# Attention's small products visit TensorE two head pairs at a time, and the first stage's plan counts blocks of instructions

## The chip, the core and the metric

The kernel runs on one core of a Trainium2 chip. Five engines work side by side there and meet through semaphores: TensorE (PE in the profile; its weight loads are shown apart as PEld), VectorE (DVE), ScalarE (ACT), GpSimd (POOL) and SyncE (SP), which issues the transfers from and to HBM. The metric is the time of one execution on the device in microseconds (us). The kernel before took 953.29, 954.51 and 958.97 us in three runs; the median, 954.51 us, is its time.

## The reference: what is computed

Attention with a narrow window over 8 batches, 8 heads, 576 positions and 64 features, followed by a feed-forward layer with a GELU:

```
scores = scale * np.matmul(q, k.transpose(0, 1, 3, 2))
mask_plain = (rel >= 0) & (rel < window)                                              # window = 32
mask_dil = (rel >= 0) & (rel < window * dilation) & (rel % dilation == 0)             # dilation = 4
attn = np.exp(scores - max) ;  attn = attn / (np.sum(attn, axis=-1, keepdims=True) + 1e-09)
x = (attn @ v), heads side by side: 4608 tokens of 512 features
h = x @ w_in                                 # 512 -> 2048
g = 0.5 * h * (1.0 + erf(h / sqrt(2)))
out = g @ w_out                              # 2048 -> 512
```

The first four heads use the plain window, the last four the dilated one; in a dilated head the positions are sorted by their remainder, so that its window is narrow too. Attention is little arithmetic in many small products, the feed-forward layer much arithmetic in large ones.

## The kernel before

**Tiling.** The tokens are worked in nine chunks of 512. Chunks 0 to 7 take the first 512 positions of a batch each; chunk 8 takes the 64 remaining positions of all eight batches. A chunk has four *head pairs* (two plain, two dilated). For a pair, `scores` multiplies blocks of 32 queries by 64 keys (L310), `lowest` and `softmax` make the exponentials on DVE and ACT, `norm` and `turn` divide and transpose on DVE, `av` multiplies by the values in products of 32 columns (L459; L451 for the dilated pairs of chunk 8, called *wide*, with 96 keys a query), and `xout` brings the result out of PSUM as two float32r parts, the value rounded by an ACT cast (L487) and the remainder by a DVE subtraction (L490).

The feed-forward layer keeps all weights in SBUF, each as two float32r parts. `ffn_h` (L501) and `ffn_o` (L516) run three products for every product of the reference, 128 rows by 512 columns each. Such a row of twelve products is called a *unit* below; a chunk has 16 units of `ffn_h` and 16 of `ffn_o`, 384 products in all.

A product of `scores` or `av` has float32 operands, and the trace shows it as two MATMULs and two LDWEIGHTS; a product of the feed-forward layer and a transpose on PE are one of each. So the row `x128` of the built program below is `x256` in the trace for small products, and `x128` is `x128` for large ones.

**The order in chunks 1 to 8** is written by hand. While the feed-forward layer of chunk c runs, the attention of chunk c+1 is put between its units by a list of steps, each with a position: position 2 is behind the second `ffn_h` unit, and from 24 to 32 a position counts quarters, three `ffn_o` products each. `A_SC` gives the position of `scores` for all four pairs, `A_X` that of `av`. So PE gets two *visits* of attention in a chunk: the scores of four pairs, 128 products one behind the other, and the value products of four pairs, 128 products or, for chunk 8, 64 and 192 wide ones.

**The first stage** (attention of chunks 0 and 1, splitting of the weights, feed-forward layer of chunk 0) is ordered by `Plan`. A job gives the engine and an estimated time of each of its steps; `Plan.run` takes, again and again, the step that can begin first by its own clock, shifted by a rank (`RANK`), and writes it into its engine's queue. `ORDER` is the order of the loads on SP. A weight arrives as 64-bit floats and is split by DVE in five or six instructions (L213 to L227) and by one ACT cast (L232). A weight in `TWICE` is loaded a second time, two bytes further on (`mid_w`), and needs one instruction less on DVE (L217). Of the first `HALVED` weights each half is split by itself.

On PE the first stage also has `turn_pe` (transposes of chunk 1, L399), `av_one` (value products of chunk 1, L413) and, for chunk 0, `av` in another shape (L429).

Of the kernel before, what the change touches and what calls it, by code (L numbers as in the profile page):

```python
# [18 lines left out]
P = 128  # L19
# [14 lines left out]
TWICE = (1, 2, 4, 7, 11, 12, 15)  # L34

HALVED = 2
# [3 lines left out]
LATE, LATE_PE, COLD = 0.25, 0.55, 38  # L40
KAPPA, AHEAD = 2.4e-05, 5
ORDER = ("q0 q1 Q0 q2 w0 q3 Q1 v0 m1 v2 m2 Q2 w1 w3 w2 w4 V0 m4 Q3 w8 w6 w5 w9 m7 w7 w11 V2 w10 m11 w14 w12 "
         "m12 w13 m15 w15")
RANK = dict(att0=-3340, split=10720, high=-3120, gelu=-7400, o=7030, scores=(-220, 1980), low=(-4680, -3170, -1270,
            -280), exp=(-220, -170, 2700, 1170), norm=(2990, 750, 2180, -840), t=(2990, 3130, 2240, 1480), av=(-7400,
            -7240), x=(-5520, -2430, -1090, -4980), store=5000)


class Plan:
# [5 lines left out]
    def __init__(self, rings):  # L55
        self.rings = {n: [0.0] * k for n, k in rings.items()}
        self.jobs, self.done, self.free = [], {}, {"DMA": 1.9}
        self.table = "exp"

# [16 lines left out]

    def run(self):
        while self.jobs:
            best = None
            for j in self.jobs:  # L80
# [7 lines left out]
                for n, t in ops.items():  # L88
                    e, _, table = n.partition("/")
                    at = max(r - (LATE if j.get("on") == e != "PE" else 0.0), self.free.get(e, 0.0))  # L90
                    end = at + t + (1.3 if table not in ("", self.table) else 0.0)
                    if e == "PE" and at < COLD:
                        end += 0.6 * t
                    choices.append((end, at, e, table))
                end, at, e, table = min(choices)
                key = (round(at + KAPPA * j["rank"], 2), j["rank"])
                if best is None or key < best[0]:
                    best = (key, j, e, at, end, table)
            _, j, e, at, end, table = best
# [18 lines left out]
def at_once(gen):  # L118

    e = None  # L120
    try:
        while True:
            e = next(iter(gen.send(e))).partition("/")[0]
# [5 lines left out]
def attn_ffn(ctx: ExitStack, tc: tile.TileContext, qk, qk_lp, qk_ld, v_0, v, v_ld, w, outT):  # L129
# [12 lines left out]
    masks = const.tile([P, NU + 1, 2 * KB], F32, name="masks")  # L142
    two_masks = const.tile([P, KL], F32, name="two_masks")
# [145 lines left out]
    def scores(s, bank):  # L289

        yield {"PE": 0.75}
# [21 lines left out]
    def lowest(s):  # L313
# [8 lines left out]
        if s.c < 2:  # L322
            yield {"DVE": 0.6}
            nc.vector.tensor_reduce(s.st[:, 0].rearrange("p (h u) -> p h u", h=2),  # L324
                                    s.sc[:, :, s.at:s.at + n].rearrange("p h (u k) -> p h u k", u=NU), axis=AX.X, op=ALU.max)
            yield {"DVE": 0.08}
# [22 lines left out]
    def softmax(s):  # L349
        for i in range(2 * NU):  # L350
            if i % 4 == 0 and s.c == 0 or i == 0:
                yield {"ACT/exp": 1.32 if s.c == 0 else 2.64}
# [4 lines left out]

    def norm(s, on="DVE"):
        t = s.st[:, 1]
        yield {"DVE": 0.08}  # L360
        nc.vector.tensor_scalar_add(t, t, EPS)
        yield {"DVE": 0.1}
        nc.vector.reciprocal(t, t)
# [4 lines left out]
        elif on == "ACT":  # L368
            yield {"ACT": 1.6}
# [25 lines left out]
    def turn_pe(s, bank):  # L395

        yield {"PE": 0.9}
# [402 lines left out]
```

## Time and profile before

| | |
|---|---|
| time, median of 3 runs | 954.51 us (953.29 to 958.97) |
| the profiled execution | 953.56 us, its span 951.8 us |
| PE busy | 889.0 us, 93% of the span, 8408 MATMULs |
| DVE, ACT busy | 359.5 us (38%), 373.6 us (39%) |
| POOL busy | 9.6 us (1%) |
| HBM | 62.91 MB read, 9.44 MB written, 76 GB/s over the span |
| chain that ended last | PE 88%, issue 4%, ACT 3%, DVE 3%, DMA 1% |

The profile's times are of one execution. In a row of the timeline the first number is the start of a group of instructions in us from the span's start, the second the group's length; at its end, in brackets, stand the idle time ahead of it and what ended that. "issue" there means that the engine waited for nothing that the profile shows. The length of a group holds the modelled end of its last product, so what a row of products costs is read from start to start. PEclk is the share of TensorE's clock that the throttle granted. A busy share is a mean over the span; what the change is worth is read place by place.

The first stage lasts to about 152.6 us, where the first two `ffn_h` units of chunk 1 begin. The chunks 1 to 7 follow with some 100 us each, and chunk 8, beside which no attention stands, ends at 948.1 us.

### The profile page before, as it was taken

The numbers are of one execution on the slowest core, as the hardware profiler recorded it, in microseconds if no ns is written. First come the engines' busy times: TensorE is split into PE (matmuls) and PEld (weight loads), VectorE is DVE, ScalarE is ACT, GpSimd is POOL, SyncE is SP. The second block draws the span as 40 slices with busy tenths as digits, with TensorE's granted clock in tenths as the row PEclk, the third lists the DMA queues.
The fourth block names the chain that finished last, engine by engine and source line by source line (L and its number), as shares of the span: only waits on it lengthen the run. The fifth ranks groups of instructions, "written<-read, shape, count | busy, mean of one in ns | idle before, by whom it ended". The sixth has DMA issues, their size and how long they took to land.

```text
span 951.8 us, 19064 instructions
## 1 busy us (share of the span) xinstructions
PE 889.0 (93%) x8408; PEld 733.4 (77%) x8408; DVE 359.5 (38%) x608; ACT 373.6 (39%) x1017; POOL 9.6 (1%) x48
## 2 busy tenths in 40 slices
PE   4588997999999999999999999999999999989998
PEld 3367886888878877887788778877787888778886
DVE  3597991362136212622163205421462155211020
ACT  5458442453236422732272316331443254323040
POOL 4000000000000000000000000000000000000000
PEclk9579999999999999999999999999999999979999
DMA  9962415000320032003300140005000430000001
GB/s 374 390 245 93 176 64 214 9 0 2 132 91 1 1 123 101 1 1 112 112 1 1 54 170 1 1 3 186 35 0 2 144 133 24 2 24 22 1 1 45
DMA packets 16643, 73.58 MB, mean 77 GB/s; under 512 B 1840, under 2 KB 2096, under 8 KB 12336
## 3 DMA queue, kind: packets, MB, share of 16 engines
q1 hardware_dynamic: 16560, 72.36, 20.7%
q8 instruction: 66, 1.08, 0.5%
q14 instruction: 17, 0.14, 0.0%
HBM read 62.91 MB, written 9.44 MB: 76 GB/s over the span
## 4 chain that ended last, share of the span: by engine, by line
PE 88%; issue 4%; ACT 3%; DVE 3%; DMA 1%; POOL 0%; SPq 0%; POOLq 0%; ACTq 0%; DVEq 0%
PE ps L516 41%; PE ps L501 40%; PE ps L459 3%; PE ps L310 3%; ACT sm L355 1%; DMA raw_qk<-qk 1%; PE ps L429 1%; PE ps L451 1%; DMA raw_w<-w 0%; PE ps L296 0%; DVE raw_w L221 0%; DVE weight L227 0%; DVE st L324 0%; DVE x L490 0%; ACT x L487 0%
## 5 line engine op out<-in xcount | busy, mean ns | idle before, releaser
L501 PE MATMUL ps<-x,weight 128*128 128x512 f32 x1728 | 408.3, 396 | 7.6 <-ACT weight L232 7.6
L516 PE MATMUL ps<-g,weight 128*128 128x512 f32 x1728 | 408.5, 396 | 0.0
L501 PEld LDWEIGHTS ps<-x,weight 128*128 128x128 f32 x1728 | 329.8, 191 | 78.3 <-ACT weight L232 8.5
L516 PEld LDWEIGHTS ps<-g,weight 128*128 128x128 f32 x1728 | 329.9, 192 | 69.8
L511 DVE TENSOR_TENSOR g<-gf,g 128x512 fp32r<-128x512 f32 x144 | 99.6, 692 | 432.7 <-ACT g L509 432.7
L506 ACT ACTIVATE gf<-ps 128x512 f32<-128x512 f32 x144 | 86.1, 598 | 336.1 <-PE ps L501 335.9
L509 ACT CAST g<-gf 128x512 fp32r<-128x512 f32 x144 | 89.4, 621 | 4.6
L355 ACT ACTIVATE sm<-sm,st 128x64 f32<-128x64 f32 (+1 forms) x224 | 74.9, 337 | 0.1
L185 ACT COPY o_sb<-ps 128x512 f32<-128x512 f32 (+1 forms) x35 | 20.3, 581 | 124.5 <-PE ps L516 123.7
L490 DVE TENSOR_TENSOR x<-ps,x 128x512 fp32r<-128x512 f32 (+1 forms) x40 | 31.7, 809 | 87.2 <-ACT x L487 78.3
L487 ACT CAST x<-ps 128x512 fp32r<-128x512 f32 (+1 forms) x40 | 29.5, 771 | 78.8 <-PE ps L459 38.1
L310 PE MATMUL ps<-raw_qk 64*32 64x64 f32 (+1 forms) x2304 | 31.3, 239 | 17.4 <-issue 15.2
L392 DVE STREAM_TRANSPOSE turned<-sm 32x256 f32<-32x256 f32 x104 | 45.4, 436 | 2.0
L310 PEld LDWEIGHTS ps<-raw_qk 64*32 64x32 f32 x2304 | 26.5, 111 | 23.6 <-issue 21.6
L355 ACT ACTIVATION_READ_ACCUMULATOR sm<-sm,st 128x1 f32 x224 | 42.1, 188 | 0.0
L459 PE MATMUL ps<-turned,v_sb 64*64 64x32 f32 x1664 | 28.1, 223 | 7.7 <-issue 7.7
L459 PEld LDWEIGHTS ps<-turned,v_sb 64*64 64x64 f32 x1664 | 26.7, 138 | 10.7 <-issue 10.7
L232 ACT CAST weight<-raw_w 128x1024 fp32r<-128x1024 f32 (+1 forms) x18 | 18.8, 1051 | 15.3 <-DVE raw_w L221 15.3
L355 ACT ACTIVATE sm<-ps,st 128x64 f32<-128x64 f32 x64 | 19.0, 329 | 7.2 <-PE ps L310 5.7
L387 DVE STREAM_TRANSPOSE turned<-sm 128x512 f32<-128x512 f32 x30 | 21.3, 710 | 0.9
L374 DVE TENSOR_TENSOR sm<-sm,st 128x512 f32<-128x512 f32 x30 | 20.7, 692 | 1.0
L221 DVE SCALAR_TENSOR_TENSOR raw_w<-raw_w,spare 128x1024 uint32<-128x1024 uint32 (+1 forms) x18 | 19.9, 1105 | 0.5
(51 smaller groups left out, 238.8 us busy)
## 6 DMA issues: line engine op xcount, KB each, us to landing
raw_qk<-qk SPq DMA_DIRECT2D x32, 512.0 KB, 6.0
raw_w<-w SPq DMA_DIRECT2D x16, 1024.0 KB, 8.0
v_sb<-v SPq DMA_DIRECT2D x15, 1024.0 KB, 5.0
outT<-o_sb SPq DMA_DIRECT2D x35, 256.0 KB, 2.2
mid_w<-w SPq DMA_DIRECT2D x7, 1023.5 KB, 6.4
raw_qk<-qk_ld SPq DMA_DIRECT2D x2, 1024.0 KB, 7.7
v_wide<-v_ld SPq DMA_DIRECT2D x2, 768.0 KB, 6.3
v<-v SPq DMA_DIRECT2D x2, 640.0 KB, 13.3
```

The costliest lines, as they stand in the source:

```text
L310: nc.tensor.matmul(s.sc[32 * r:32 * r + 32, h, c0:c0 + s.nk], x[:, q0:q0 + 32], x[:, k0:k0 + s.nk], start=s.c > 1, stop=s.c > 1 or u == NU ...
L355: nc.scalar.activation(t, s.sc[:, i // NU, at:at + 2 * KB] if s.c < 2 else t, AF.Exp, bias=s.st[:, 0, i:i + 1], scale=SCALE if s.c < 2 els ...
L387: nc.vector.transpose(s.t.rearrange("p i j b -> p (i j b)"), s.all.rearrange("p i k -> p (i k)"))
L392: nc.vector.transpose(s.t[32 * to:32 * to + 32, :, r % 2], s.all[32 * r:32 * r + 32, :, j * KB:(j + 1) * KB])
L459: nc.tensor.matmul(px(r)[h * D:(h + 1) * D, u * KB:(u + 1) * KB], s.v[rows, u, j, h * D:(h + 1) * D], s.t[rows, h * NU + slot(s, u), j], s ...
L487: nc.scalar.copy(h, y)
L490: nc.vector.tensor_sub(l, y, h)
L501: nc.tensor.matmul(bank, weights[f][:, t, cc * P:(cc + 1) * P], x[:, xx], start=n == 0, stop=n == 3 * NC - 1)
L506: nc.scalar.activation(gf, bank, AF.Gelu)
L509: nc.scalar.copy(g[:, 0], gf)
L511: nc.vector.tensor_sub(g[:, 1], gf, g[:, 0])
L516: nc.tensor.matmul(ps[:, d], weights[f][:, t, DM + d * P:DM + (d + 1) * P], gs[f][:, u], start=f == 0 and n == 0, stop=f == NF - 1 and n == 2)
```

## The change

Three things are changed.

1. In chunks 1 to 7 the attention steps are spread over more visits. `scores` of pairs 0 and 1 stays at position 2, that of pairs 2 and 3 goes to position 4; `av` of pairs 0 and 1 stays at 24.75, that of pairs 2 and 3 goes to 26.75, and their `xout` behind it. The wide `av` of chunk 8 is cut in halves of 96 MATMULs (`u0`), 18 or 3 feed-forward products apart. `lowest`, `softmax`, `norm`, `turn` and the loads keep their positions.
2. `Plan` has another model of PE: `on_pe` counts instructions in blocks of 256, lets a block be there a fixed time after the block ahead of it began, and makes PE slower for 4.5 us after a pause. Steps on PE give their number of instructions ("PE:132"). Some estimated times on DVE and ACT are new, and the sum and its inverse are a step of their own (`inverse`).
3. `TWICE` now has ten weights (3, 5, 6, 7, 8, 10 to 14) instead of seven (1, 2, 4, 7, 11, 12, 15), `HALVED` is 3 instead of 2, and `ORDER` and `RANK` have other entries. `gate` is new but not reached: `ORDER` has no entry that begins with n.

```
-TWICE = (1, 2, 4, 7, 11, 12, 15)
+TWICE = (3, 5, 6, 7, 8, 10, 11, 12, 13, 14)
-HALVED = 2
+HALVED = 3
-LATE, LATE_PE, COLD = 0.25, 0.55, 38
+BLOCK, FIRST, FETCH, FETCH_BUSY = 256, 63, 4.2, 5.9
+SLOW, WARM, IDLE = 0.8, 4.5, 1.5
-ORDER = ("q0 q1 Q0 q2 w0 q3 Q1 v0 m1 v2 m2 Q2 w1 w3 w2 w4 V0 m4 Q3 w8 w6 w5 w9 m7 w7 w11 V2 w10 m11 w14 w12 "
+ORDER = ("q0 q1 Q0 q2 v2 q3 Q1 m5 w2 v0 w0 w1 w3 w4 Q2 Q3 V0 V2 m3 w5 w7 m7 m6 m10 w6 m8 w9 w8 m11 w12 m13 w10 "
...
+    def on_pe(self, at, t, n, keep):
+        busy = at if at - self.free.get("PE", 0.0) > IDLE else self.busy
+        there, count, begin = dict(self.there), self.n, at
+        while n > 0:
+            k = count // BLOCK
+            begin = max(begin, there[k])
+            if k + 1 not in there:
+                there[k + 1] = begin + (FETCH if self.free["DMA"] < begin + 1 else FETCH_BUSY)
+            some = min(n, (k + 1) * BLOCK - count)
+            d = t * some / n
+            begin, t = begin + d * (1 + (SLOW if begin < busy + WARM else 0)), t - d
+            count, n = count + some, n - some
+        if keep:
+            self.there, self.n, self.busy = there, count, busy
+        return begin
...
-        yield {"PE": 0.75}
+        yield {"PE:132": 1.15}
...
-    def av(s, px):
+    def av(s, px, u0=0):
...
-            for u in range(NU):
+            for u in range(u0, u0 + 2):
...
-    A_SC, A_LOW, A_E, A_N, A_X, A_QK, A_V = 2, 2.5, 8.5, 10.5, 24.75, 26.5, 3
+    A_SC, A_E, A_N, A_X, A_QK, A_V = (2, 4), 8.5, 10.5, (24.75, 26.75), 26.5, 3
...
-            add(c, A_SC if not wide else 8.25, 1, scores(s[p], bank))
-            add(c, A_LOW + p if not wide else 8.5 + (p - 2), 2, lowest(s[p]))
+            add(c, A_SC[p // 2] if not wide else 8.25, 1, scores(s[p], bank))
+            add(c, A_SC[p // 2] + .5 + p % 2 if not wide else 8.5 + (p - 2), 2, lowest(s[p]))
...
-            add(c, A_X, 6, av(s[p], px[0]))
-            add(c, A_X + .25 + p / 2, 7, xout(s[p], px[1]))
+            at = A_X[p // 2] + (1.75 * (p - 2) if wide else 0)
+            for u in (range(0, NU, 2) if wide else [0]):
+                add(c, at + .75 * u, 6, av(s[p], px[0], u))
+            add(c, at + (1.75 if wide else .25 + p % 2 / 2), 7, xout(s[p], px[1]))
```

**A whole chunk on PE.** These are PE's rows of chunk 2 in the built program of the kernel before (any of the chunks 1 to 6 reads the same); L501 and L516 are the feed-forward layer, L310 the scores, L459 the value products.

```order
L501 MATMUL ps<-x,weight 128x512 x24
L310 MATMUL ps<-raw_qk 32x64 x128
L501 MATMUL ps<-x,weight 128x512 x72
L516 MATMUL ps<-g,weight 128x512 x96
L501 MATMUL ps<-x,weight 128x512 x96
L516 MATMUL ps<-g,weight 128x512 x9
L459 MATMUL ps<-turned,v_sb 64x32 x128
L516 MATMUL ps<-g,weight 128x512 x87
```

And this is the same chunk in the changed program, whose lines are L533 and L548, L339 and L491.

```order
L533 MATMUL ps<-x,weight 128x512 x24
L339 MATMUL ps<-raw_qk 32x64 x64
L533 MATMUL ps<-x,weight 128x512 x24
L339 MATMUL ps<-raw_qk 32x64 x64
L533 MATMUL ps<-x,weight 128x512 x48
L548 MATMUL ps<-g,weight 128x512 x96
L533 MATMUL ps<-x,weight 128x512 x96
L548 MATMUL ps<-g,weight 128x512 x9
L491 MATMUL ps<-turned,v_sb 64x32 x64
L548 MATMUL ps<-g,weight 128x512 x24
L491 MATMUL ps<-turned,v_sb 64x32 x64
L548 MATMUL ps<-g,weight 128x512 x63
```

Each of the two visits of 128 products became two of 64 with two feed-forward units, 24 products, between them; nothing is added.

**The value products of chunk 8 on PE**, which stand in chunk 7. Before (L451 are the wide ones):

```order
L516 MATMUL ps<-g,weight 128x512 x9
L459 MATMUL ps<-turned,v_sb 64x32 x64
L451 MATMUL ps<-turned,v_wide 64x32 x192
L516 MATMUL ps<-g,weight 128x512 x87
L501 MATMUL ps<-x,weight 128x512 x96
```

Now (L483 are the wide ones):

```order
L548 MATMUL ps<-g,weight 128x512 x9
L491 MATMUL ps<-turned,v_sb 64x32 x64
L548 MATMUL ps<-g,weight 128x512 x24
L483 MATMUL ps<-turned,v_wide 64x32 x48
L548 MATMUL ps<-g,weight 128x512 x18
L483 MATMUL ps<-turned,v_wide 64x32 x48
L548 MATMUL ps<-g,weight 128x512 x3
L483 MATMUL ps<-turned,v_wide 64x32 x48
L548 MATMUL ps<-g,weight 128x512 x18
L483 MATMUL ps<-turned,v_wide 64x32 x48
L548 MATMUL ps<-g,weight 128x512 x24
```

One visit of 256 products became five.

**The first stage on PE.** Before, from the second `ffn_o` unit on; ahead of it stand three `ffn_h` units, one `ffn_o` unit, eight transposes (L399), the first value products of chunk 1 and its second scores.

```order
L516 MATMUL ps<-g,weight 128x512 x12
L501 MATMUL ps<-x,weight 128x512 x12
L516 MATMUL ps<-g,weight 128x512 x12
L501 MATMUL ps<-x,weight 128x512 x12
L516 MATMUL ps<-g,weight 128x512 x12
L501 MATMUL ps<-x,weight 128x512 x12
L516 MATMUL ps<-g,weight 128x512 x12
L399 MATMUL ps<-early,sm 128x128 x4
L501 MATMUL ps<-x,weight 128x512 x12
L399 MATMUL ps<-early,sm 128x128 x4
```

Now, from the first `ffn_o` unit on; ahead of it stand three `ffn_h` units, no `ffn_o` unit, and the same attention work.

```order
L548 MATMUL ps<-g,weight 128x512 x12
L533 MATMUL ps<-x,weight 128x512 x12
L548 MATMUL ps<-g,weight 128x512 x24
L533 MATMUL ps<-x,weight 128x512 x12
L431 MATMUL ps<-early,sm 128x128 x4
L548 MATMUL ps<-g,weight 128x512 x12
L431 MATMUL ps<-early,sm 128x128 x4
L533 MATMUL ps<-x,weight 128x512 x12
L445 MATMUL ps<-turned,v_sb 64x32 x64
L548 MATMUL ps<-g,weight 128x512 x12
```

The sixth `ffn_h` unit (the third L501 of the first fence, the third L533 of the second) has four `ffn_o` units ahead of it in the first fence, one of them ahead of the fence, and four in the second. The second eight transposes (L399, now L431) moved from behind the sixth `ffn_h` unit to ahead of it.

More of the change, by code (lines that the diff above doesn't have):

```diff
@@ L58, in __init__ @@
         self.table = "exp"
+        self.n, self.there, self.busy = FIRST, {0: 0.0, 1: 0.0}, 0.0
     def add(self, name, gen, after=(), take=(), give=(), rank=0, delay=0.15):
@@ L87, in run @@
                 choices = []
-                for n, t in ops.items():
-                    e, _, table = n.partition("/")
+                for what, t in ops.items():
+                    name, _, table = what.partition("/")
+                    e, _, n = name.partition(":")
                     at = max(r - (LATE if j.get("on") == e != "PE" else 0.0), self.free.get(e, 0.0))
[L91 to L95, printed above, removed]
+                    if e == "PE":
+                        end = self.on_pe(at, t, int(n), False)
+                    else:
+                        end = at + t + (1.3 if table not in ("", self.table) else 0.0)
+                    choices.append((end, at, e, table, t, n))
+                end, at, e, table, t, n = min(choices)
                 key = (round(at + KAPPA * j["rank"], 2), j["rank"])
                 if best is None or key < best[0]:
-                    best = (key, j, e, at, end, table)
-            _, j, e, at, end, table = best
+                    best = (key, j, e, at, end, table, t, n)
+            _, j, e, at, end, table, t, n = best
+            if e == "PE":
+                self.on_pe(at, t, int(n), True)
             self.table = table or self.table
@@ L122, in at_once @@
         while True:
-            e = next(iter(gen.send(e))).partition("/")[0]
+            e = next(iter(gen.send(e))).partition("/")[0].partition(":")[0]
     except StopIteration:
@@ L351, in softmax @@
             if i % 4 == 0 and s.c == 0 or i == 0:
-                yield {"ACT/exp": 1.32 if s.c == 0 else 2.64}
+                yield {"ACT/exp": 1.2 if s.c == 0 else 2.4}
             t = s.sm[i // NU][:, i % NU]
@@ L356, in softmax, with inverse @@
                                  scale=SCALE if s.c < 2 else -1.0, accum_out=s.st[:, 1, i:i + 1])
+    def inverse(s):
+        t = s.st[:, 1]
+        yield {"DVE": 0.2}
+        nc.vector.tensor_scalar_add(t, t, EPS)
+        yield {"DVE": 0.24}
+        nc.vector.reciprocal(t, t)
     def norm(s, on="DVE"):
         t = s.st[:, 1]
[L360 to L363, printed above, removed]
         if s.wide:
@@ L368, in norm @@
         elif on == "ACT":
-            yield {"ACT": 1.6}
+            yield {"ACT": 1.95}
             for i in range(2 * NU):
@@ L564, in load_of @@
             dma(("wmid", i), w_load_mid(raws[i], i), ["w"])
+        elif what == "n":
+            gate(i)
         elif what in "qQ":
@@ L570, in load_of, with gate, gen @@
             dma(("v", c, i), load_v(xs[c][i]), ["w"])
+    def gate(i):
+        def gen():
+            yield {"DMA": 0.05}
+            nc.sync.dma_start(gates[0:1, i:i + 1], xs[0][i].st[0:1, 1, 0:1])
+        dma(("gate", i), gen(), [], [("sums", 0, i)], 0.0)
     loads = ORDER.split()
```

43 lines of the change are left out of this document (24 added, 19 removed).

## The prediction

> **What bounds the kernel now.** I read the chain that ended last first, then who waits for whom, then PE's timeline. The chain is PE's own:
>
> ```profile
> PE 88%; issue 4%; ACT 3%; DVE 3%; DMA 1%; POOL 0%; SPq 0%; POOLq 0%; ACTq 0%; DVEq 0%
> ```
>
> The list of waits says what the 4% of "issue" are (total, times, longest):
>
> ```profile
> PE ps L310 <- issue: 15.2, 7, 3.4
> PE ps L459 <- issue: 7.7, 6, 1.4
> PE ps L451 <- issue: 5.6, 3, 2.3
> PE ps L310 <- DMA raw_qk<-qk: 2.2, 4, 0.9
> ```
>
> PE's timeline shows where they lie and how far apart:
>
> ```profile
> 22.91 0.70 PE L310 MATMUL ps<-raw_qk 64*32 64x64 f32 x45 [1.93 <-issue]
> ...
> 152.60 5.60 PE L501 MATMUL ps<-x,weight 128*128 128x512 f32 x24
> ...
> 235.75 1.28 PE L459 MATMUL ps<-turned,v_sb 64*64 64x32 f32 x37 [1.20 <-issue]
> 236.97 22.64 PE L516 MATMUL ps<-g,weight 128*128 128x512 f32 x87
> ...
> 264.97 2.71 PE L310 MATMUL ps<-raw_qk 64*32 64x64 f32 x236
> 269.74 0.56 PE L310 MATMUL ps<-raw_qk 64*32 64x64 f32 x20 [2.05 <-issue]
> ...
> 729.73 3.35 PE L459 MATMUL ps<-turned,v_sb 64*64 64x32 f32 x214
> 734.46 0.83 PE L459 MATMUL ps<-turned,v_sb 64*64 64x32 f32 x42 [1.39 <-issue]
> 735.22 20.02 PE L516 MATMUL ps<-g,weight 128*128 128x512 f32 x87
> 755.07 5.60 PE L501 MATMUL ps<-x,weight 128*128 128x512 f32 x24
> 760.60 1.48 PE L310 MATMUL ps<-raw_qk 64*32 64x64 f32 x128
> 762.01 16.64 PE L501 MATMUL ps<-x,weight 128*128 128x512 f32 x72
> 778.49 0.84 PE L516 MATMUL ps<-g,weight 128*128 128x512 f32 x3
> 779.26 1.79 PE L310 MATMUL ps<-raw_qk 64*32 64x96 f32 x128
> 780.98 21.38 PE L516 MATMUL ps<-g,weight 128*128 128x512 f32 x93
> 802.20 21.92 PE L501 MATMUL ps<-x,weight 128*128 128x512 f32 x96
> 823.96 2.20 PE L516 MATMUL ps<-g,weight 128*128 128x512 f32 x9
> 826.09 2.07 PE L459 MATMUL ps<-turned,v_sb 64*64 64x32 f32 x128
> 828.09 1.07 PE L451 MATMUL ps<-turned,v_wide 32*64 32x32 f32 x85
> 830.77 1.47 PE L451 MATMUL ps<-turned,v_wide 32*64 32x32 f32 x128 [1.61 <-issue]
> 834.50 2.04 PE L451 MATMUL ps<-turned,v_wide 32*64 32x32 f32 x128 [2.26 <-issue]
> 838.23 0.92 PE L451 MATMUL ps<-turned,v_wide 32*64 32x32 f32 x43 [1.69 <-issue]
> 839.08 21.97 PE L516 MATMUL ps<-g,weight 128*128 128x512 f32 x87
> 860.89 21.92 PE L501 MATMUL ps<-x,weight 128*128 128x512 f32 x96
> ```
>
> In the long wide visit a gap comes after every 128 MATMULs, which with their 128 weight loads are 256 instructions, and PE resumes at 830.77, 834.50 and 838.23: every 3.73 us. So instructions come in blocks of 256, and the next block is there some 3.73 us after the one ahead began. 256 feed-forward instructions last 29 us, 256 small ones 1.5 to 2 us. A visit of 512 small ones therefore runs dry once; the two visits of 256 at 760.60 and 779.26 don't wait at all.
>
> The gaps cost a second time, in the clock. Two stretches of the view by windows (length, PE, PEld, DVE, ACT and POOL busy, granted clock, share of DMA, GB/s), one with a gap and one with an unbroken visit:
>
> ```profile
> 231.00:241.00 10.00, 8.80 (x267) 7.66 (x267) 1.65 (x4) 2.25 (x3) 0.00 (x0) 0.74 0.01 3
> 762.00:780.00 18.00, 18.00 (x141) 14.74 (x140) 6.88 (x13) 7.36 (x13) 0.00 (x0) 1.00 0.33 117
> ```
>
> The 87 products behind the first take 22.64 us (236.97), behind the undisturbed visit at 729.73 only 20.02.
>
> **The chunks: what they cost and will cost.** Chunks 1 to 6 stand between 152.60 and 755.07: 602.47 us. Chunk 7 takes 860.89 − 755.07 = 105.82. A feed-forward product is (823.96 − 802.20)/96 = 0.2267 us, so the 384 of a chunk are 87.04.
>
> An unbroken scores visit: 762.01 − 760.60 = 1.41; ahead of it 24 products took 5.53 instead of 5.44, behind it 72 took 16.48 instead of 16.32. Sum 1.66. An unbroken value visit: 828.09 − 826.09 = 2.00; ahead of it 9 products took 2.13 instead of 2.04, and behind such a visit 87 took 19.85 (735.22 to 755.07) instead of 19.72. Sum 2.22. A new chunk 1 to 6 has two of each: 87.04 + 3.32 + 4.44 = 94.80; six are 568.8. In chunk 1 the keys come late (the 2.2 us of DMA above); the first visit needs two of the four tiles. I leave it 1.3, the second has two units more to wait in. So 570.1 instead of 602.47: **−32.4 us**.
>
> Chunk 7: scores 1.66; wide scores 1.72 (779.26 to 780.98) + 0.09 + 0.14 = 1.95; values 2.22; four wide visits of 96 at 1.07/85 = 0.0126 each, 1.21 + 0.22 = 1.43, together 5.72. Sum 98.6 instead of 105.82: **−7.2 us**. Chunk 8 stays.
>
> Of these 39.6 us the gaps are 15.2 + 7.7 + 5.6 less the 1.93 at 22.91, which lies in the first stage: 26.6, and DMA 0.9. Sixteen more visits (two more in each of six chunks, four in chunk 7) cost 16 × 0.23 = 3.7. The rest, 15.8, is the clock.
>
> Will the new visits run dry? In the old scores visit the block ended after 236 MATMULs (264.97), so the one before ended after 108. The number of PE instructions ahead hardly changes, so this holds in the new first visit: the block that begins there has 20 small MATMULs (0.2 us), 24 products (5.4), and 84 small ones of the second visit (0.9): 6.6 us against 3.73. The block before it had 20 products and 108 small ones, 5.7. Values: the end at 214 of 256 puts one at 86 in the first visit; then 42 small (0.7), 24 products, 62 small (1.0): 7.1 us. The tightest is chunk 7: 21 wide, 3 products, 96 wide, 8 products, about 4.6 us. Where transfers run, loading may take longer; the longest gap, 3.4 us in chunk 1, is the upper end, with the 6.6 us as cover.
>
> Each visit changes the array's tiling twice, and there are 32 more such changes. [...]
>
> The later `xout` now waits for a later visit. On ACT only copies of results for the store are queued behind it. Its rows:
>
> ```profile
> L490 DVE TENSOR_TENSOR x<-ps,x 128x512 fp32r<-128x512 f32 (+1 forms) x40 | 31.7, 809 | 87.2 <-ACT x L487 78.3
> L487 ACT CAST x<-ps 128x512 fp32r<-128x512 f32 (+1 forms) x40 | 29.5, 771 | 78.8 <-PE ps L459 38.1
> ```
>
> The last wide visit has 24 products (5.4 us) behind it before the next chunk reads x; two casts and two subtractions of such lengths, overlapping, need about 2.4. Nothing is late. Without that cover it would be some 2 us, once. Scores of pairs 2 and 3 are read by DVE at the same positions as before.
>
> **The first stage.** Here PE's order changes, and DVE's loads with it. Its rows around the sixth `ffn_h` unit:
>
> ```profile
> 85.08 4.61 PE L501 MATMUL ps<-x,weight 128*128 128x512 f32 x12 [2.90 <-ACT weight L232]
> 89.53 2.92 PE L516 MATMUL ps<-g,weight 128*128 128x512 f32 x12
> 92.29 0.60 PE L399 MATMUL ps<-early,sm 128*128 128x128 f32 x4
> 92.64 3.02 PE L501 MATMUL ps<-x,weight 128*128 128x512 f32 x12
> ...
> 75.05 0.17 DVE L361 TENSOR_SCALAR st<-st 128x8 f32<-128x8 f32 x1 [3.67 <-ACT sm L355]
> 78.23 1.22 DVE L217 SCALAR_TENSOR_TENSOR raw_w<-raw_w 128x1024 uint32<-128x1024 uint32 x1
> ```
>
> After 85.08 PE waits for nothing until chunk 1; it waited for a weight before. As long as the sixth unit starts where it does, the rest is PE's own sum. Ahead of that unit stand nine units in both programs. Among the first six weights three were loaded twice and now two are: one L217 more, +1.2 us on DVE; one more weight in halves is under a microsecond. Against it DVE had 3.67 us of waiting there, which the new order may fill. I take no change at 85.08, with −5 (that wait and some of PE's own filled) and +5 (DVE's additions, and one weight's chain of ACT and DVE, unhidden) as ends. Behind it two groups of transposes are gone, 2 × 0.35 (92.29 to 92.64), and the slow clock of the sixth unit, 4.45 (85.08 to 89.53) instead of 2.72, need not recur; a block may run dry behind the second value products, which no row shows, 0 to 1.4, and I take the upper end. Together **−1.0 us**. The later weights, eight loaded twice instead of four, relieve DVE where PE doesn't wait for it: nothing.
>
> **Sum.** 953.56 − 39.6 − 1.0 = 913.0 for such an execution. That of before was 0.95 below its median, so I forecast **914 us**, 4.2% less.
>
> **Rivals.**
>
> *The clock stays low.* If the small products themselves, not the gaps, bring the clock down, the 15.8 us don't come: 914 + 15.8 = 930. For: every clock loss stands next to a visit. Against: 1.00 through both unbroken visits (762:780). [...] Chance 0.08.
>
> *The blocks lie otherwise.* If one visit in each of six chunks begins right with a block, 3.73 − 1.41 = 2.3 us of waiting return in each, 14 us: 928. The changed first stage would have to shift the count by over a hundred instructions. Chance 0.05.
>
> *The first stage turns worse.* PE waits once more for a weight behind ACT and DVE, twice the 2.90 at 85.08 and the slow clock behind it (1.7 each): +9, 923. For: DVE's order is wholly new. Chance 0.09.
>
> *Slower than before.* If a block's loading does not run beside feed-forward products but starts when its first instruction is due, each of the 31 new visits waits 3.73: 914 + 116 = 1030. It decides above (39.6 + 1.0)/31 = 1.3 us a visit. The visits at 760.60 and 779.26 speak against it, each with a block's end and no wait. Chance 0.02.
>
> The forecast itself has 0.76. Its own bounds are −5 and +5 from the first stage and ±2 from the visits: 907 to 921. With the worse first stage **906 to 924** holds 8 in 10. A measurement here tells 1% from no change, some 9.5 us: all cases but the last are faster by more. Faster 0.97, same 0.01, slower 0.02.
>
> **What would show it.** "issue" on L339, L491 and L483 near zero except in the first stage; chunks 2 to 6 at 94.8 us each; 24 products behind a visit within 0.2 us of 5.44; a granted clock of 1.00 from chunk 2 on; chunk 1's first `ffn_h` at 151.6. Gaps that are left inside visits of 128 MATMULs, or slow runs of products without a gap ahead, would make it wrong.

## The result, and the profile after

The changed kernel takes **910.46 us** (median; 910.32 to 911.40), 0.954 of the time before (95% interval 0.950 to 0.958; with a fourth run of the kernel before, its median is 953.9 us). The profiled execution took 910.51 us with a span of 908.4 us. The chain that ended last is now nearly all PE:

```profile
PE 92%; DVE 3%; ACT 2%; issue 1%; DMA 1%; POOL 0%; SPq 0%; POOLq 0%; ACTq 0%
```

In its list of waits (total, times, longest) only these three rows have to do with instruction blocks or late keys. The two of "issue" lie in the first stage, the third in chunk 1:

```profile
PE ps L461 <- issue: 4.8, 2, 3.5
...
PE ps L339 <- issue: 2.7, 1, 2.7
...
PE ps L339 <- DMA raw_qk<-qk: 0.9, 1, 0.9
```

L491 and L483, whose predecessors waited 7.7 and 5.6 us, have no row any more. PE's timeline shows the beginning of chunk 1, the visits of chunk 2, and the two ends of chunk 7:

```profile
149.42 5.60 PE L533 MATMUL ps<-x,weight 128*128 128x512 f32 x24
154.95 0.86 PE L339 MATMUL ps<-raw_qk 64*32 64x64 f32 x64
156.68 0.86 PE L339 MATMUL ps<-raw_qk 64*32 64x64 f32 x64 [0.88 <-DMA raw_qk<-qk]
...
245.32 5.60 PE L533 MATMUL ps<-x,weight 128*128 128x512 f32 x24
250.85 1.48 PE L339 MATMUL ps<-raw_qk 64*32 64x64 f32 x128
252.27 5.76 PE L533 MATMUL ps<-x,weight 128*128 128x512 f32 x24
257.95 1.48 PE L339 MATMUL ps<-raw_qk 64*32 64x64 f32 x128
...
316.05 2.07 PE L491 MATMUL ps<-turned,v_sb 64*64 64x32 f32 x128
318.05 5.74 PE L548 MATMUL ps<-g,weight 128*128 128x512 f32 x24
323.72 2.07 PE L491 MATMUL ps<-turned,v_sb 64*64 64x32 f32 x128
325.72 14.58 PE L548 MATMUL ps<-g,weight 128*128 128x512 f32 x63
340.13 5.60 PE L533 MATMUL ps<-x,weight 128*128 128x512 f32 x24
...
719.39 5.60 PE L533 MATMUL ps<-x,weight 128*128 128x512 f32 x24
...
817.58 12.63 PE L533 MATMUL ps<-x,weight 128*128 128x512 f32 x55
```

No bracket stands behind a visit but the one in chunk 1, and chunk 2 lasts 340.13 − 245.32 = 94.81 us. The granted clock is whole, here right behind a value visit; around one it was 0.74 before (view by windows, same columns as above):

```profile
231.00:241.00 10.00, 10.00 (x44) 8.27 (x45) 2.16 (x2) 3.32 (x4) 0.00 (x0) 1.00 0.50 191
```

Where the 43.05 us between the two profiled executions come from, read from start to start:

| part | before | after | difference | forecast |
|---|---|---|---|---|
| to chunk 1 | 152.60 | 149.42 | −3.2 | −1.0 |
| chunks 1 to 6 | 602.47 | 569.97 | −32.5 | −32.4 |
| chunk 7 | 105.82 | 98.19 | −7.6 | −7.2 |
| chunk 8 and outside the span | 92.67 | 92.93 | +0.3 | 0 |

The first row is known only to about a microsecond: in eight profiled executions of this first stage, the experiments' included, chunk 1 begins between 148.94 and 150.39 us, and in two of the old one at 152.60 and 153.16.

Before varied more from run to run than after (951.4 to 959.0 against 910.3 to 911.4). One experiment below bears on the reason.

### The profile page after: what moved, and what is told of

It reads as the page before. It is cut to its first block, busy times and chain, and to the rows that moved or that the text cites. A ratio compares the mean times of both kernels' runs of the same rounds, so it can differ in the third digit from the quotient of the medians.

```text
span 908.4 us, 19090 instructions
## 1 busy us (share of the span) xinstructions
PE 873.2 (96%) x8408; PEld 718.9 (79%) x8408; DVE 357.9 (39%) x612; ACT 370.9 (41%) x1016; POOL 9.6 (1%) x48
## 3 DMA queue, kind: packets, MB, share of 16 engines
q8 instruction: 66, 1.08, 0.5%
## 4 chain that ended last, share of the span: by engine, by line
PE 92%; DVE 3%; ACT 2%; issue 1%; DMA 1%; POOL 0%; SPq 0%; POOLq 0%; ACTq 0%
PE ps L548 42%; PE ps L533 42%; PE ps L339 3%; PE ps L491 3%; ACT sm L384 1%; PE ps L461 1%; PE ps L325 1%; DMA raw_qk<-qk 1%; DVE raw_w L250 1%; PE ps L483 0%; DVE x L522 0%; DVE raw_w L246 0%; DVE st L353 0%; DVE weight L256 0%; ACT x L519 0%
## 5 line engine op out<-in xcount | busy, mean ns | idle before, releaser
L533 PE MATMUL ps<-x,weight 128*128 128x512 f32 x1728 | 404.5, 392 | 4.2 <-ACT weight L261 4.2
L548 PE MATMUL ps<-g,weight 128*128 128x512 f32 x1728 | 402.3, 391 | 0.0
L533 PEld LDWEIGHTS ps<-x,weight 128*128 128x128 f32 x1728 | 324.5, 189 | 74.1 <-ACT weight L261 5.2
L548 PEld LDWEIGHTS ps<-g,weight 128*128 128x128 f32 x1728 | 322.7, 188 | 67.4 <-issue 0.2
L339 PEld LDWEIGHTS ps<-raw_qk 64*32 64x32 f32 x2304 | 26.4, 114 | 10.5 <-issue 9.3
L339 PE MATMUL ps<-raw_qk 64*32 64x64 f32 (+1 forms) x2304 | 30.9, 245 | 3.5 <-issue 2.7
L491 PEld LDWEIGHTS ps<-turned,v_sb 64*64 64x64 f32 x1664 | 25.4, 135 | 4.6 <-issue 4.6
L491 PE MATMUL ps<-turned,v_sb 64*64 64x32 f32 x1664 | 26.9, 220 | 0.0
L256 DVE SCALAR_TENSOR_TENSOR weight<-raw_w,spare 128x1024 fp32r<-128x1024 uint32 (+1 forms) x19 | 20.1, 1058 | 0.9
```

What stands on the lines that cost most here:

```text
L339: nc.tensor.matmul(s.sc[32 * r:32 * r + 32, h, c0:c0 + s.nk], x[:, q0:q0 + 32], x[:, k0:k0 + s.nk], start=s.c > 1, stop=s.c > 1 or u == NU ...
L491: nc.tensor.matmul(px(r)[h * D:(h + 1) * D, u * KB:(u + 1) * KB], s.v[rows, u, j, h * D:(h + 1) * D], s.t[rows, h * NU + slot(s, u), j], s ...
L533: nc.tensor.matmul(bank, weights[f][:, t, cc * P:(cc + 1) * P], x[:, xx], start=n == 0, stop=n == 3 * NC - 1)
L548: nc.tensor.matmul(ps[:, d], weights[f][:, t, DM + d * P:DM + (d + 1) * P], gs[f][:, u], start=f == 0 and n == 0, stop=f == NF - 1 and n == 2)
```

## Experiments

**Each half of the change by itself.** First the kernel before with the visits split and its own first stage:

```
-    A_SC, A_LOW, A_E, A_N, A_X, A_QK, A_V = 2, 2.5, 8.5, 10.5, 24.75, 26.5, 3
+    A_SC, A_E, A_N, A_X, A_QK, A_V = (2, 4), 8.5, 10.5, (24.75, 26.75), 26.5, 3
...
+            for u in (range(0, NU, 2) if wide else [0]):
+                add(c, at + .75 * u, 6, av(s[p], px[0], u))
```

> The first stage as before, the visits as changed. If the chunks' gain comes from the visits alone, the chunks take what they take in the changed kernel (95.9 for chunk 1, 94.8 for each of chunks 2 to 6, 98.2 for chunk 7) and chunk 1 begins at 152.6 as before: 910.5 + 3.2 = 913.7 us. Rival: the new plan is needed for the gain, because it sets where the blocks of instructions lie in the chunks; then gaps of 1 to 2 us stay in some chunks and the time is 920 or more.

Measured: 914.37 us, ratio 0.9621 [0.9585, 0.9657], as expected. Chunk 1 begins at 153.16, and chunks 2 to 6 last 94.81 each. Then the other half, the changed first stage with the old visits (the same lines the other way round in the changed kernel):

> The new first stage, the visits as before. If the two parts add up, chunk 1 begins at 149.4 as in the changed kernel, and the chunks 1 to 7 are as long as before, with the same gaps: 953.6 - 3.2 = 950.4 us. Rival: the first stage's gain is lost or doubled in chunk 1, where the keys come late: 3 us either way.

Measured: 948.36 us, ratio 0.9969 [0.9936, 1.0002]. By its time alone this half can't be told from no change; the profiled run starts chunk 1 at 148.94, near the 149.4 of the expectation. The gaps are all there again:

```profile
PE ps L339 <- issue: 15.7, 7, 3.9
PE ps L491 <- issue: 8.2, 6, 1.6
...
PE ps L483 <- issue: 4.7, 3, 1.7
```

So the visits bring the bulk by themselves and the first stage some 3 to 4 us. What follows a gap varies much. These are the 87 products behind the value visits of chunks 1 to 3 in this run:

```profile
234.72 21.27 PE L548 MATMUL ps<-g,weight 128*128 128x512 f32 x87
...
333.96 20.04 PE L548 MATMUL ps<-g,weight 128*128 128x512 f32 x87
...
432.38 21.42 PE L548 MATMUL ps<-g,weight 128*128 128x512 f32 x87
```

The slow clock follows a gap in some chunks and not in others. The gap's length doesn't decide it: in the kernel before, gaps of 1.39 us were followed by 87 products in 21.18 us once (635.97; granted clock 0.95 from 636 to 660) and in 20.02 us once (735.22; 1.00 from 736 to 760). With the gaps went the scatter: the split visits alone ran within 1.5 us, this kernel within 8.8.

**Do the block ends have to lie well?** The prediction counted from the moment in which PE *executes* the first instruction of a block. By that count a visit that begins right with a block must wait 2.3 us. 103 products of 128 columns (206 instructions, their result unused) are added in chunk 1 of the changed kernel, so that in chunks 2 to 6 a block ends ten to two instructions into the first scores visit:

```
+            for i in range((13 if f < NF - 1 else 12) if c == 1 else 0):
+                nc.tensor.matmul(ps[:, 6, 0:P], weights[0][:, 0, 0:P], weights[0][:, 0, 0:P], start=True, stop=True)
```

> The changed kernel with 103 added products of 128 columns (206 instructions) among the ffn_h units of the second half of chunk 1, whose results nobody reads. They cost some 7 us in chunk 1 and move every later block of 256 instructions, so that the first scores visit of chunks 2 to 6 begins 10, 8, 6, 4 and 2 instructions before a block does, that of chunk 7 right with one. Theory of the blocks: the next block is due 5, 4, 3, 2 and 1 feed-forward products behind that visit and 3.73 us after the last one began; PE waits there, behind the visit and not in it, 1.0, 1.2, 1.4, 1.6 and 1.9 us (2.1 in chunk 7), and nowhere else; the chunks 2 to 6 take 95.8 to 98.5, more where the clock drops. Rival, the length of a visit decides (PE runs dry after some 110 small products in a row, wherever they stand): no wait, 94.8 each. For the clock: if waits bring it down, it drops in some of these chunks; if the small products do, it stays at 1.00 as in the changed kernel, since they are the same.

Measured: 922.9 us, in one run. Some 11 us of it are the added products themselves (0.108 each, in chunk 1; 7 us were expected). **The expectation of waits failed:** the waits of "issue" are those of the first stage and no other, and chunks 2 to 6 last 94.81 as before, as the expectation's rival had it. So the count from execution was wrong, though the forecast built on it was right.

**The price of a visit.** One head pair a visit, eight visits a chunk:

```
+    A_SC, A_E, A_N, A_X, A_QK, A_V = (2, 3, 4, 5), 8.5, 10.5, (24.75, 25.75, 26.75, 27.75), 26.5, 3
...
```

> The changed kernel with one head pair a visit: eight visits of 64 MATMULs in a chunk instead of four of 128 (the wide ones as they are), one unit apart for the scores, 12 products for the values; the reductions of pairs 0 and 2 on DVE one position later. Theory: no gap, and every visit costs 0.22 to 0.25 us for changing the tiling and back, so 0.92 more a chunk: chunks 2 to 6 95.7 each, in all 910.5 + 6 x 0.92 + 0.46 = 916.5 us. Rival: the price hangs on the products, not on the visits: 910.5. [...]

Measured: 919.06 us, ratio 0.9672 [0.9636, 0.9708], 2.6 us above the expectation. Chunk 2 lasts 341.75 − 245.49 = 96.26, 1.45 more than with four visits: 0.36 for each added visit, not 0.23. From chunk 2 on nothing waits. A visit costs more than the two slow edges that the prediction read: 32 products take 0.79 us where 64 took 1.41.

**When does a block's loading begin?** The view of transfers has the answer. The page gives the instruction queue a row of its own (transfers, MB, share of 16 engines):

```profile
q8 instruction: 66, 1.08, 0.5%
```

1.08 MB in 66 transfers is 16 KB each. The trace has 8408 MATMULs and 8408 weight loads, 255 instructions for each transfer, so I take one transfer for one block of 256. In the kernel before, the view of the transfers between 827 and 837 us, where the wide visit runs dry, has 40 slices of 0.25 us:

```profile
GB/s 0 0 0 0 66 0 0 0 0 0 0 0 0 0 0 0 0 0 0 66 0 0 0 0 0 0 0 0 0 0 0 0 0 0 66 0 0 0 0 0
...
q8 instruction: 3, 0.05, 2.3%
```

The transfers begin at about 828.0, 831.8 and 835.6, the last two some 1.1 us after PE resumed (830.77, 834.50 in the prediction's rows), and PE resumes 2.7 us after a transfer began: the 3.73 us. In the same view between 749 and 752 us (slices of 0.075), beside feed-forward products:

```profile
GB/s 0 0 0 0 0 0 0 0 0 0 0 0 0 0 0 0 0 218 0 0 0 0 0 0 0 0 0 0 0 0 0 218 382 382 382 437 355 382 300 328
...
q8 instruction: 1, 0.02, 2.6%
```

This transfer begins at 750.3. Counted from the block that PE resumed with at 734.46 (42 small MATMULs and 86 products, two instructions each), the next block is first executed at about 754.8. That block's own transfer had come long before, at 735.6, again 1.1 us after PE resumed; the one at 750.3 is that of the block behind it. It lies 4.5 us ahead of 754.8, and its cause, if it is again 1.1 us earlier, 5.6 us ahead: by this estimate 25 products, about 50 instructions. So here a block's loading started ahead of the execution of the block before it. That instructions are handed to PE some 50 ahead of their execution, and that the handing over of a block's first one starts the loading of the next, is inferred from these times; no view shows the handing over. In the run with the shifted count the transfer lies likewise 3.7 us ahead of the visit into which the block was to end (259.6 against 263.27), so that shift did what it should.

This makes a new theory, A: 50 instructions ahead are 5.6 us beside feed-forward products and 0.3 us inside a visit. By it, a visit of one block behind feed-forward products can't run dry, wherever the block ends; one of two blocks runs dry unless a block ends in its first 15 to 30 instructions, an estimate from these figures. B is the old count from execution, C the rule that a visit must not be longer than a block. Whole visits of 128 products tell them apart. Without and with a shift of the block ends:

```
-    A_SC, A_E, A_N, A_X, A_QK, A_V = (2, 4), 8.5, 10.5, (24.75, 26.75), 26.5, 3
+    A_SC, A_E, A_N, A_X, A_QK, A_V = (3, 3), 8.5, 10.5, (24.75, 24.75), 26.5, 3
...
```

```
+            for i in range(40 if (c, f) == (1, 0) else 0):
+                nc.tensor.matmul(ps[0:32, 6, 0:32], diag.bitcast(F32)[0:64, 0:32], diag.bitcast(F32)[0:64, 0:32], start=True, stop=True)
```

> The same whole visits without the added products: the first block end lies 195 instructions behind the start of a scores visit and 184 behind that of a values visit. A: PE waits 3.73 - 320 x 0.0056 = 1.9 in the scores and 3.73 - 320 x 0.00785 = 1.2 in the values, 3.1 a chunk. B and C: 2.3 and 1.7, 4.0 a chunk. With the slow clock that such waits bring in some chunks: 924 to 945, by every theory; what tells is the difference to the run with the added products.

> The four score visits and value visits of a chunk are made two again, as before the change: all four head pairs' scores in one visit of 128 products behind the fourth ffn_h unit (not the third) and all values in one of 128; the last chunk's wide values stay in halves. Forty products of 64 rows and 32 columns (160 instructions, 0.022 us each) are added in chunk 1 and write a PSUM area that nobody reads; they move the ends of the instruction blocks to 35 instructions behind the start of a scores visit and 24 behind that of a values visit. [...] Each chunk has two visits less, 94.8 - 2 x 0.23 to 0.36 = about 94.2; chunk 1 also loses its 0.88 us wait for the keys and pays 0.9 + 0.25 for the added products: 910.5 - 6 x 0.6 - 0.4 - 0.9 + 1.15 = about 907. Theory B (a block counts from its first execution, as the prediction had it): a scores visit's full block lasts 256 x 0.0056 = 1.4 us, so PE waits 2.3 there, and 3.73 - 256 x 0.00785 = 1.7 in the values visit: 4.0 a chunk, 931, with the clock up to 945. Theory C (visits must be no longer than a block): the same waits as in B.

Without the shift 935.92 us (one run), with it 911.18 (ratio to before 0.9569 [0.9536, 0.9602]), 4 us above the expectation. The added products, all in one tile position, took 2.71 us instead of 0.9. A third run bought the shift in a wait of the first stage, in four column groups, where they took 0.92 us:

```
+    def shift():
+        yield {"PE:0": 0.0}
+        for i in range(42):
+            r = 32 * (i % 4)
+            nc.tensor.matmul(ps[r:r + 32, 5, 0:32], diag.bitcast(F32)[0:64, 0:32],
+                             diag.bitcast(F32)[0:64, 0:32], start=True, stop=True)
...
```

> Whole visits as in the run with the forty added products, but the shift of the block ends is bought elsewhere: 42 products of 64 rows and 32 columns (168 instructions), in four column groups, stand in the first stage ahead of the second scores of chunk 1, where PE waits 4.67 us for bank 6, and write the bank of the next ffn_h unit, which that unit overwrites. The values visit stands one feed-forward product group (6 instructions) earlier. The first block end then lies 27 to 22 instructions behind the start of a scores visit (chunk 1 to 6), and 22 to 17 behind that of a values visit. Theory A, with the depth that the last runs showed (loading begins 40 to 50 instructions ahead of the block's execution): the load for the second end starts 1.5 to 3 us ahead of the scores visit and is there 0.7 to 2.2 us into it, where the end is due at 1.6: no wait over 0.5 us; in the values none. Chunks 2 to 6 last 94.02 as the chunk 5 of the last run instead of 94.81, chunk 1 also loses its 0.88 us wait for the keys; the added products lie in a wait: 910.5 - 6 x 0.79 - 0.9 = about 905. Theory B (from first execution): 2.3 + 1.7 us of waits a chunk, 929 or more.

Measured: 908.63 us, ratio 0.9536 [0.9507, 0.9565]. PE's timeline without the shift, chunks 1 and 2:

```profile
225.98 3.46 PE L491 MATMUL ps<-turned,v_sb 64*64 64x32 f32 x220
230.51 0.77 PE L491 MATMUL ps<-turned,v_sb 64*64 64x32 f32 x36 [1.07 <-issue]
...
259.32 2.42 PE L339 MATMUL ps<-raw_qk 64*32 64x64 f32 x225
263.88 0.53 PE L339 MATMUL ps<-raw_qk 64*32 64x64 f32 x31 [2.14 <-issue]
264.33 15.41 PE L533 MATMUL ps<-x,weight 128*128 128x512 f32 x60
```

and with the free shift:

```profile
158.29 1.64 PE L339 MATMUL ps<-raw_qk 64*32 64x64 f32 x142
161.94 1.64 PE L339 MATMUL ps<-raw_qk 64*32 64x64 f32 x114 [2.01 <-issue]
...
223.35 3.94 PE L491 MATMUL ps<-turned,v_sb 64*64 64x32 f32 x256
227.21 20.70 PE L548 MATMUL ps<-g,weight 128*128 128x512 f32 x90
247.75 8.32 PE L533 MATMUL ps<-x,weight 128*128 128x512 f32 x36
256.00 2.73 PE L339 MATMUL ps<-raw_qk 64*32 64x64 f32 x256
258.66 13.90 PE L533 MATMUL ps<-x,weight 128*128 128x512 f32 x60
...
341.77 8.32 PE L533 MATMUL ps<-x,weight 128*128 128x512 f32 x36
```

The same unbroken visits of 512 instructions wait in one program and not in the other; only the block ends lie otherwise. Chunk 2 now lasts 341.77 − 247.75 = 94.02, shorter than with four visits by 0.79, and chunks 3 to 6 are the same. The transfers of the two kernels show the reason. Without the shift, from 260 to 264 us (slices of 0.1), the block's transfer begins at 261.1, 1.8 us *into* the visit of 259.32:

```profile
GB/s 0 0 0 0 0 0 0 0 0 0 0 164 0 0 0 0 0 0 492 82 82 0 164 492 82 82 82 82 328 573 164 410 737 164 410 655 164 492 573 246
...
q8 instruction: 1, 0.02, 2.0%
```

With it, from 252 to 258 us (slices of 0.15), it begins at about 254.3, some 1.7 us *ahead* of the visit of 256.00, and nothing waits for it:

```profile
GB/s 601 164 655 218 601 273 546 273 219 0 0 0 0 0 0 109 0 0 0 0 0 0 0 0 0 0 0 0 0 0 0 0 0 0 0 0 0 0 0 0
...
q8 instruction: 1, 0.02, 0.9%
```

B and C fall: by both, the whole visits had to wait in either program. A's own forecast held for 11 of the 12 whole visits of this run. The time is 3.6 us above A's 905, because chunk 1 took 97.72 us: its scores visit waits 2.01 us. The run before it has 1.52 us there, and 0.76 and 0.19 us behind the scores visits of chunks 2 and 3.

A doesn't give these waits, but other transfers lie beside each of them. The unshifted run shows what that does, since its chunks 1 and 2 have the same order on PE. In chunk 2 nothing but the block is transferred from 257.5 to 261.5; its transfer begins 1.8 us behind the start of the scores visit, and PE waits 2.14. In chunk 1 the visit starts at 158.53 and the transfer begins 3.8 us behind it, at 162.3, and PE waits 3.61. Until then the loads of data fill the DMA engines; this is their queue from 159.5 to 162.3, with its share of the 16 engines last:

```profile
q1 hardware_dynamic: 176, 1.18, 100.0%
```

So here a block's transfer began some 2 us later (3.8 against 1.8), where other transfers filled the engines. The prediction allowed for that (its 3.4 us in chunk 1), and the planner of the changed kernel counts with it (5.9 instead of 4.2 us). That the waits of the shifted runs have this cause is argued from where they lie and was not tried by itself. For chunk 1's scores visit another cause stays open: its keys were requested from 152.0 to 153.4 and took 4.0 to 6.7 us to land; whether a wait for them also put off the block's loading, no run shows.

The last variant keeps four visits and puts the second value visit 3 products behind the first, so that 518 instructions stand nearly together:

```
+    A_SC, A_E, A_N, A_X, A_QK, A_V = (2, 4), 8.5, 10.5, (24.75, 25), 26.5, 3
```

> The changed kernel with the second value visit 3 products behind the first instead of 24: 64 MATMULs, 3 products, 64 MATMULs. The first block ends 183 instructions into the first visit. A: from the handing over of that block to its end pass 137 x 0.00785 + 0.68 + 177 x 0.00785 = 3.15 us: a wait of 0.6 a chunk, about 914. B: 0.57 + 0.68 + 1.39 = 2.64, a wait of 1.1 a chunk, about 917. C: each visit is one block long, no wait, 910.5.

Measured: 915.92 us, in one run. In PE's timeline of chunk 1:

```profile
225.88 1.52 PE L491 MATMUL ps<-turned,v_sb 64*64 64x32 f32 x89
227.66 0.78 PE L491 MATMUL ps<-turned,v_sb 64*64 64x32 f32 x39 [0.26 <-issue]
```

Five of the six chunks have such a wait, 0.25 to 0.48 us, 1.8 in all: below A's 0.6, and well below B's 1.1. C had no wait. Read from start to start, chunks 2 to 6 are 0.2 to 0.8 us longer than 94.81, 2.6 in all. The rest of the 5.5 us above 910.46 lies elsewhere: chunk 1 begins 1.0 later and is 1.3 longer, with 1.6 us of waits for its keys instead of 0.9. So the time, between A's 914 and B's 917, decides nothing; the waits speak for A and against C. What matters is the feed-forward work between visits, not the length of one.

**Which part of the planner's model gives the first stage?** Its block costs and its slow clock were taken away one at a time, with list and ranks as they are:

```
-BLOCK, FIRST, FETCH, FETCH_BUSY = 256, 63, 4.2, 5.9
+BLOCK, FIRST, FETCH, FETCH_BUSY = 256, 63, 0.0, 0.0
```

> The changed kernel with the planner's two costs for the loading of an instruction block set to nothing (its list of loads and its ranks as they are). Only the first stage's order changes. If the block count carries the first stage's gain, chunk 1 begins 1 to 4 us later than 149.42 and the time is 911.5 to 915; if the list and the ranks carry it, 910.5 within half a microsecond.

```
-SLOW, WARM, IDLE = 0.8, 4.5, 1.5
+SLOW, WARM, IDLE = 0.0, 4.5, 1.5
```

> The changed kernel with the planner's cost for PE's slow start set to nothing (its block costs, its list and its ranks as they are): the other half of what its plan counts anew. Only the first stage's order changes. If both counts are needed for the gain of the first stage, chunk 1 begins 1 to 4 us later than 149.42 and the time is 911.5 to 915; if the block count alone carries it, 910.5 within one microsecond either way.

Without block costs 914.64 us (0.9607 [0.9574, 0.9640]), without the slow clock 907.75 (0.9529 [0.9498, 0.9560]). In the first, PE waits behind the sixth `ffn_h` unit for the transposes' operand, the `ffn_o` unit behind them takes 4.59 us instead of some 3, and chunk 1 begins 4.0 us later than in the changed kernel:

```profile
88.13 0.33 PE L431 MATMUL ps<-early,sm 128*128 128x128 f32 x1 [1.83 <-ACT sm L403]
...
153.43 5.60 PE L533 MATMUL ps<-x,weight 128*128 128x512 f32 x24
```

In the second it begins 3.05 us earlier:

```profile
146.37 5.60 PE L533 MATMUL ps<-x,weight 128*128 128x512 f32 x24
```

The expectation for the block costs held, at its upper end. That for the slow clock missed on both branches: with this list and these ranks, this part of the model costs some 3 us. The list and ranks were not fitted anew to either, so the two runs tell what each cost does in this order, not what it is worth at best.

**Chunk 1's wait for its keys.** Both scores visits of chunk 1 one unit later:

```
-            add(c, A_SC[p // 2] if not wide else 8.25, 1, scores(s[p], bank))
+            add(c, A_SC[p // 2] + (c == 1) if not wide else 8.25, 1, scores(s[p], bank))
...
```

> The changed kernel with both scores visits of chunk 1 one ffn_h unit later, which the wait for the keys (0.88 us at 156.68) lies ahead of; the order of PE's instructions is otherwise the same. If that wait is the whole cost, chunk 1 goes from 95.90 to 95.0 and the time to 909.6; if the work moved later is late for the values, 910.5 or more.

Measured: 909.44 us, ratio 0.9548 [0.9517, 0.9579], as expected, and no wait for keys is left in the list. Chunk 1 takes 94.77 us instead of 95.90. The wait of 0.88 had cost 1.1: in the changed kernel the visit around it took 2.52 us (154.95 to 157.47) instead of 1.41. The clock had no part in it, since the 24 products behind that visit took 5.67 us there and 5.68 in chunk 2.

**What helped, together:** the plan without the slow clock, whole visits with their block ends placed, chunk 1's scores split and one unit later.

```
-SLOW, WARM, IDLE = 0.8, 4.5, 1.5
+SLOW, WARM, IDLE = 0.0, 4.5, 1.5
...
+            plan.add(("scores",) + k, both(([shift()] if p else []) + [scores(s, 6), scores(t, 6)], 2.3, 264),
...
+    A_SC, A_E, A_N, A_X, A_QK, A_V = (3, 3), 8.5, 10.5, (24.5, 24.5), 26.5, 3
...
+            add(c, A_SC[0] + (p // 2 * 2 if c == 1 else 0) if not wide else 8.25, 1, scores(s[p], bank))
...
```

> What helped in the last runs, together: the plan without the cost for the slow clock (907.75); whole scores visits in chunks 2 to 6 and whole values visits in chunks 1 to 6, their block ends placed by the 42 added products ahead of the second scores of chunk 1 (in this plan PE waits 1.14 us there and they last 0.92); chunk 1's scores in two visits, one ffn_h unit later each, since the whole visit waited 2.01 there and the early one 1.4 for its keys. By theory A no wait from chunk 1 on: 907.75 - 5 x 0.79 (chunks 2 to 6) - 1.4 (keys) - 0.3 (one values visit of chunk 1) + 0 to 1 for the added products: 902 to 903. If the placed block ends helped by chance of that one order, waits of 2 us come back in some chunks and the time is 905 to 915.

Measured: **903.62 us** (903.25 to 904.16), ratio 0.9485 [0.9456, 0.9514], 6.8 us below the changed kernel. The two ratios' intervals just meet; the traces show the difference where it was made: chunk 1 begins 1.5 us earlier, and chunks 1 to 6 take 565.10 us instead of 569.97. From chunk 1 on its timeline has one wait left, again in chunk 1's scores:

```profile
147.95 8.32 PE L533 MATMUL ps<-x,weight 128*128 128x512 f32 x36
...
165.02 0.33 PE L339 MATMUL ps<-raw_qk 64*32 64x64 f32 x10 [0.35 <-issue]
```

The time is 0.6 to 1.6 above the expectation: chunk 1 begins 1.6 later than without the added products. Some 0.5 of it is there ahead of them already; then the unit ahead of them took 4.85 us instead of 3.28 and left no wait for them to fill.

## Why the prediction was right, and where not

*The chunks: right, size and reason.* 94.80 for a new chunk came out as 94.81; chunk 1 at 245.32 − 149.42 = 95.90 against 94.80 + 1.3; chunk 7 at 98.19 against 98.6. A sum made of rows that already showed an unbroken visit with its edges needed no model of the hardware.

*The split of the 39.6 us: partly wrong.* The 26.6 of gaps are gone; of DMA waits 1.3 went (2.2 to 0.9), not 0.9. The price of 0.23 for one more visit was too small. Half visits cost 0.36 more each, and taking two of four visits away gave 0.79, 0.40 each. At these prices 16 visits cost 5.8 to 6.4 instead of 3.7, and the remainder, which the forecast called the clock, is 18.0 to 18.6 instead of 15.8. Not all of it is the clock. Read from start to start in the trace before, the products behind the visits ran some 12 us longer than behind unbroken ones. Some 6 us more lie in the broken visits themselves, over and above the gaps as listed: the one at 729.73 lasts 5.49 us to 735.22, an unbroken one 3.86 (223.35 to 227.21), and only 1.39 of the difference of 1.63 is listed. The total was safe because price and remainder were taken from the same rows.

*The clock: right, though one row was misread.* It is 1.00 from chunk 1 on (149 to 900 in the trace after), and the visits themselves don't bring it down. In the unshifted run 60 products behind a 2.14 us gap took 15.41 us (granted clock 0.83 from 264 to 274), behind the unbroken visit of the shifted one 13.90 (1.00 from 256 to 270). But the visit at 729.73 was not undisturbed, as the forecast said: its own next row has a gap of 1.39 us. The granted clock stayed at 1.00 there (729 to 735 and 735 to 755), so the price taken from it held; it was luck that the gap did not matter. The window 762:780 lies between the two unbroken visits; 760:762 and 779:781, on them, show 1.00 too.

*Will the new visits run dry: right answer, wrong count.* The 6.6, 5.7 and 7.1 us of cover were counted from a block's first execution. In the trace before, a transfer began 4.5 us ahead of that execution (750.3 against 754.8), so the cover was larger than counted, and the rival in which the blocks lie otherwise didn't have the 2.3 us a chunk that it was given: the shifted count made it happen and nothing waited. The rival on the other side, loading that starts when its first instruction is due, fell with it. The expectations count A's waits with a lead of 320 − 256 instructions, which no run shows; the transfer at 750.3 gives about 50, and the waits themselves were 1.07 and 2.14 us in the whole visits without the shift and 0.25 to 0.48 us in the close value visits.

*The first stage: the mis-sized term.* −1.0 was forecast, −3.2 measured. Of the 3.5 us between the forecast and 910.46 these are 2.2; the chunks and the end give 0.3, and 1.0 comes from the median, which was to lie 0.95 above the profiled execution and lies on it. These rows answer to those of the sixth `ffn_h` unit before:

```profile
81.33 3.00 PE L548 MATMUL ps<-g,weight 128*128 128x512 f32 x12
84.17 0.60 PE L431 MATMUL ps<-early,sm 128*128 128x128 f32 x4
84.52 2.99 PE L533 MATMUL ps<-x,weight 128*128 128x512 f32 x12
87.44 2.07 PE L445 MATMUL ps<-turned,v_sb 64*64 64x32 f32 x128
89.44 3.02 PE L548 MATMUL ps<-g,weight 128*128 128x512 f32 x12
```

The sixth unit starts at 84.52 instead of 85.08 and waits for nothing, where no change was taken: −0.56. That is within the scatter (84.02 to 85.47 in eight executions of this first stage), and that the start hardly moved is luck: the 2.90 us of waiting there are gone, but PE now waits 4.67 us at 63.03 for the second scores' bank, for which the forecast had no row. From there to chunk 1 it is 64.90 instead of 67.52, and 64.9 in all eight. The transposes and the slow clock were priced about right (−2.43 together, for −2.62). The step that failed is the 1.4 us of a dry block behind the second value products: 87.44 to 89.44 is an unbroken visit. I took the upper end of 0 to 1.4 without a row for it; by theory A one block of small products behind feed-forward work has its successor there in time.

## What to carry to other kernels

Where PE has a gap that "issue" ends, look at the instruction queue's own transfers: here PE resumed every 3.73 us where it ran dry block after block (830.77, 834.50, 838.23), a block's transfer began some 2 us later where other transfers filled the DMA engines (3.8 against 1.8 us into a visit), and beside feed-forward products the loading was set off some 50 instructions ahead (an estimate, from 750.3 against 754.8). So a run of many cheap instructions was free as long as it was no longer than one block and had 24 feed-forward products, 48 instructions, ahead of it and no heavy loads beside it (in the joined kernel one such visit, in chunk 1 with its loads, still waited 0.35 us); a longer one was free only where the block ends suited it, which 168 harmless instructions in an idle place could arrange. Take the duration of a changed piece whole from a place where the trace already has it in that shape, rather than from a price per edge.

## What the runs showed of the hardware that I had not expected

- An instruction block's loading is visible and runs ahead of the execution: beside feed-forward products its transfer began 4.5 us before the block ahead of it was executed (750.3 against 754.8), and some 1.1 us after PE resumed where PE had run dry (735.6 after 734.46).
- Beside loads that filled the DMA engines a block's transfer began 3.8 us behind the start of a visit, without them 1.8 (162.3 and 261.1 in the unshifted run), and PE waited 3.61 instead of 2.14 us.
- Two visits of 256 instructions with 24 products between never waited for a block in the changed kernel; two with 3 products between waited 0.25 to 0.48 us in five chunks of six.
- The slow clock behind a gap of 1 to 2 us comes in some chunks and not in others: behind the same value visit 87 products took 21.27, 20.04 and 21.42 us in three chunks of one run, and in the kernel before the granted clock was 0.79 around a gap of 1.08 us (434 to 442) and 1.00 around one of 1.31 (333 to 345). What decides it no run shows. That it makes the scatter of the kernel before is argued from the runs without gaps, which scatter little.
- Products of 64 rows and 32 columns cost 2.71 us for 80 MATMULs (0.034 each) in one tile position and 0.92 us for 84 (0.011 each) spread over four column groups.
